# Fourier mixing and a gated convolution on one core: tables loaded in halves, part of the weight conversion on ScalarE

## The chip, the cores and the metric

The kernel runs on one core of a Trainium2 chip. The core has a tensor engine (PE, with weight loads shown as PEld), a vector engine (DVE), a scalar engine (ACT), GpSimd (POOL) and a sync engine (SP) that here only issues transfers. Each engine works through its own instructions in order; semaphores let one wait for another. The metric is the time of one execution on the device in microseconds (us).

## The reference, cut to what matters

```python
X = np.fft.fft(x, axis=1)             # x: 8 x 3136 x 256
X = np.fft.fft(X, axis=2)
x = X.real                            # goes into the second block
h = np.maximum(x @ w_in, 0.0)         # w_in: 256 x 1024
hp = pad(h, one zero row at either end of the sequence)
for k in range(3):
    conv_out += conv_w[k] * hp[:, k:k + S, :]
gate = 1.0 / (1.0 + np.exp(-conv_out))
out = (h * gate) @ w_out              # w_out: 1024 x 256
```

The weights come in as 64-bit floats and must be turned into 32-bit ones on the chip; x is 32-bit.

## The kernel before, in words

**The transform.** The Fourier transform along the sequence is done as matrix products with cosine and sine tables. Symmetry cuts the work: a sequence is first folded (`fold_ops`, on DVE, from tiles `xh`) into sums and differences over quarters of the sequence, in two halves h = 0 and 1 of four slots q, each from its own load of x (a plain transfer and four gathered ones that read mirrored rows). The folded values lie in two tiles `wt[b]`: one for even output frequencies, one for odd. The tables lie in `tabs[0]` (even) and `tabs[1]` (odd). ACT doubles the odd table by mirroring it (`mirror_tables(q)`, two slots at a time, L239) and halves one row (`mend_row`, L233). A `Unit` is a group of products into one PSUM tile, an ACT copy out of it and DVE additions (`fin`) that write the tiles `pt` (P) and `qt` (Q) in `PQ[b]`. The first batch has four odd units whose products are issued in four parts (parts 0 and 1 use slots 0 and 1, parts 2 and 3 slots 2 and 3), then four even units and one for a single feature column.

**The weights.** The transform along the features is merged into w_in: `blocks(i)` multiplies a quarter of w_in by the table `dm` into the matrix `G` (and one row into the tile `left`), `column(i)` makes the vector `ge`. The 64-bit weights are loaded as pairs of integers and converted by `narrow` with seven DVE instructions on 512 columns (L515 to L522): exponent cut out, rebased and clamped at zero, shifted into place, sign put in, mantissa's high word with its leading bit, low word added, product. w_in is narrowed in four quarters (`w_in[0]` to `w_in[3]`), w_out in four pieces of two blocks of rows (numbered 0, 2, 4, 6). Quarters 0 and 1 of w_in share one tile and their columns interleave; so do quarters 2 and 3.

**The steps.** Then come 256 steps (b, c, f): batch, one of four chunks of the sequence, one of eight blocks of 128 of the 1024 features. The loop is software pipelined and the order of all engines is written out by hand. In turn t it issues: sigmoid of step t-2 (ACT); the products of step t+1 (PE: `pb` = Q x G, `pa` = P x G, both 128 x 386) and their copies (ACT); the combination of step t (DVE, L686) into h, front and mirrored back of the chunk; side work; the seed of `pa` for step t+2 (ACT); the first tap of step t (ACT, L692), the other two taps of step t-1 (DVE, L698), the gate of step t-2 (half on POOL, L718, half on DVE, L719); and the output products of step t-3 (PE, `po`, `mm2`). Side work is hung into named places of a turn by `at(turn, place, function)`: "pe", "act", "dve", "load".

For the first 20 steps (`triple`), the front of h is not combined on DVE: PE adds a third product, Q x G again, into `pa` after `pb` has been read as the negative part, and ACT takes the front straight from PSUM by a Relu (L672). For the first four steps (`first`), the seed is a one-row product with `left` instead of an ACT activation.

**What sets the order at the start.** x goes out first on SP's queue, half 0 and then half 1 (the second behind a small POOL memset), then the odd tables (behind another memset, L575), quarter 0 of w_in, the even tables, `dm`, the other quarters. `keep_on(n)` is n idle products on PE (L748), which fill the time before the odd units. PE's wait for DVE or ACT is a count on that engine's semaphore.

Of the kernel before, what the change touches and what calls it, by code (L numbers as in the profile page):

```python
# [26 lines left out]

TRIPLE = 20  # L30
FIRST = 4
RC = 56
NQ = 8
# [5 lines left out]
def kernel(  # L39
# [22 lines left out]
    QO = HO // 2  # L62
    NF = F // P
# [6 lines left out]
    const = ctx.enter_context(tc.tile_pool(name="const", bufs=1))  # L70
# [19 lines left out]
    stt = nc.vector.scalar_tensor_tensor  # L90
    act = nc.scalar.activation

    def mm(o, l, r, start, stop):
        nc.tensor.matmul(o, l, r, start=start, stop=stop, skip_group_check=True)  # L94
# [12 lines left out]
    sg = const.tile([P, 2, 2], F32, name="sg")  # L107
# [96 lines left out]
    tabs = [const.tile([P, n, HQ, HE], F32, name="tab%d" % n) for n in (2, 4)]  # L204
    PQ, eb, er = {}, {}, {}
    ed = edp.tile([B, (RC // 2 + 1) * RC], F32, name="ed")

    def table(k, st, q, cols):
        return tabs[st // 2][0:k, st, q, cols] if st < 2 else tabs[1][0:k, st - 2, q, cols]

    def load_tables(par):


        st = slice(2 * par, 2 * par + 2)
        to = tabs[par][:, 0:2].rearrange("p s q i -> p s (q i)")
        n = HQ * HE
        m = NP // 2 // 16 * 16
        for i in range(2):
            nc.sync.dma_start(out=to[i:2 * m:2], in_=dft_seq[0:m, st, HQ * i:HQ * (i + 1)]
                              .rearrange("p s q i -> p s (q i)"))  # L220
        assert NP == 2 * m + 2
        nc.sync.dma_start(out=to[2 * m:NP], in_=bass.AP(
            tensor=dft_seq.tensor, offset=dft_seq.offset + (m * 4 + 2 * par) * NQ * HE,
            ap=[[n, 2], [NQ * HE, 2], [1, n]]))
        nc.sync.dma_start(out=to[NP:KR], in_=bass.AP(
            tensor=dft_seq.tensor, offset=dft_seq.offset + ((NP * 4 + 2 * par) * NQ - HQ + 2) * HE,
            ap=[[n, 1], [NQ * HE, 2], [1, n]]))

    def mend_row(par, half):
# [273 lines left out]
    left = const.tile([P, NF, P], F32, name="left")  # L503
# [1 line left out]

    def narrow(dst, raw):

        ts = nc.vector.tensor_scalar  # L510
        lsl, lsr = ALU.logical_shift_left, ALU.logical_shift_right
        lo, hi = raw[:, :, :, 0], raw[:, :, :, 1]
        lof, d = lo.bitcast(F32), dst.bitcast(I32)

        ts(out=d, in0=hi, scalar1=20, scalar2=0x7FF, op0=lsr, op1=ALU.bitwise_and)  # L515
        ts(out=d, in0=d, scalar1=-896, scalar2=0, op0=ALU.add, op1=ALU.max)
        ts(out=d, in0=d, scalar1=23, scalar2=None, op0=lsl)
        stt(out=d, in0=hi, scalar=-0x80000000, in1=d, op0=ALU.bitwise_and, op1=ALU.bitwise_or)

        ts(out=hi, in0=hi, scalar1=0xFFFFF, scalar2=0x100000, op0=ALU.bitwise_and, op1=ALU.bitwise_or)  # L520
        stt(out=lof, in0=lo.bitcast(U32), scalar=2.0 ** -32, in1=hi, op0=ALU.mult, op1=ALU.add)
        stt(out=dst, in0=lof, scalar=2.0 ** -20, in1=dst, op0=ALU.mult, op1=ALU.mult)  # L522

    class Weight:

# [7 lines left out]
        def load(self, eng):  # L533
            if self.raw is None:
                eng.dma_start(out=self.dst, in_=self.src)
            else:
                eng.dma_start(out=self.raw.rearrange("p c n e -> p c (n e)"), in_=self.src)

        def narrow(self, c0, c1):
            if self.raw is not None:  # L540
                narrow(self.dst[:, c0:c1], self.raw[:, c0:c1])

    ident = gp.tile([3 * NF, 3 * NF], F32, name="ident", tag="g")
    make_identity(nc, ident)
# [73 lines left out]
    hs, gs, pa, pb, po, nb = {}, {}, {}, {}, {}, {}  # L618
# [34 lines left out]
    def products(s):  # L653
        b, c, f = s
        ch, n, fs = cut(s)
        pb[s] = psb.tile([P, 512], F32, name="pb", tag="pb")
        mm(pb[s][:, 0:n], G[0:P - 1, 1, fs], PQ[b][1][0:P - 1, ch.k0:ch.k1], True, True)
        mm(pa[s][:, 0:n], G[:, 0, fs], PQ[b][0][:, ch.k0:ch.k1], first(s), not triple(s))
        if first(s):
            mm(pa[s][:, 0:n], left[0:1, f, :], er[b][:, ch.k0:ch.k1], False, False)  # L660
        if triple(s):
            mm(pa[s][:, 0:n], G[0:P - 1, 1, fs], PQ[b][1][0:P - 1, ch.k0:ch.k1], False, True)

# [36 lines left out]
    def shares(s):  # L700

        ch = chunks[s[1]]
        w = ch.w - 2
        n = ch.rest[0] if ch.last else w
        return slice(0, n // 2), slice(n // 2, n), slice(n, w)

    def sigmoid(s):

        v, p, r = shares(s)
        for c in (slice(p.start, r.stop), v):  # L710
            act(gs[s][:, c], gs[s][:, c], AF.Sigmoid)  # L711
# [36 lines left out]
    def keep_on(n):  # L748

        for _ in range(n):  # L750
            mm(idle[:, 0:2 * P], wt[0][1][0:NP, 1, 0], wt[0][1][0:NP, 0, 0:2], True, True)
# [54 lines left out]

# [40 lines left out]
    for b in range(1, B):  # L847
        ops = fold_ops(b)
        c0, n = ends[b - 1], ends[b] - ends[b - 1]
# [12 lines left out]
    n = len(steps)  # L862
# [4 lines left out]
    for t in range(n + LAG):  # L867
        def run(where):
            for fn in side.get((t, where), []):
                fn()  # L870
        if 0 <= t - 2 < n:
            sigmoid(steps[t - 2])
        if t + 1 < n:
            products(steps[t + 1])
            copies(steps[t + 1])
        run("act")
        if t < n:
            combine(steps[t])
# [12 lines left out]
        run("pe")  # L891
# [66 lines left out]
```

## Time and profile before

| what | before |
| --- | --- |
| time, median of 3 | 1218.17 us (1217.98 to 1218.82) |
| span of the profiled run | 1216.7 us |
| PE busy | 1185.4 us, 97% |
| DVE busy | 1125.0 us, 92% |
| ACT busy | 877.6 us, 72% |
| POOL busy | 373.2 us, 31% |
| chain that ended last | PE 70%, DVE 21%, issue 4%, ACT 2% |
| output products `po` on PE | 3072 passes, 380 ns mean |
| other taps (L698) on DVE | 512 instructions, 1073 ns mean |

A 32-bit matmul is run in two passes, each of which is one record; records overlap, since matmuls are pipelined, so a busy PE isn't PE at its peak. The chain that ended last is followed back from the last instruction, at each step to what released it. In the time lines a row has the start, the time it spans, engine, line, operation, output <- inputs, shape, count, and in brackets the idle time ahead of it and what ended that. Several like instructions are merged in one row. In the groups of waits, the time is that in which the waiting engine stood idle.

### The profile page before, as it was taken

Reading aid. Unit: us, or ns where it says so; the run is one execution under the profiler, and the core shown is the slowest. Engines: PE = TensorE matmul, PEld = TensorE weight load, DVE = VectorE, ACT = ScalarE, POOL = GpSimd, SP = SyncE. Lnnn points to the kernel's source line nnn. Section 1 sums busy time; section 2 is a strip of 40 time slices with the busy share of each in tenths; the row PEclk is TensorE's granted clock in tenths of the full one; section 3 lists DMA queues with packets and bytes.
Section 4 is the critical chain, followed back from the end, with each engine's and each line's share of the span. In section 5 each row is a group of like instructions: output and inputs, shape, how many; then the busy total and the mean of one; then the engine's idle time right before and its main releaser. Section 6 shows DMA issues by size and latency. Waiting matters only on the chain.

```text
span 1216.7 us, 15448 instructions
## 1 busy us (share of the span) xinstructions
PE 1185.4 (97%) x4876; PEld 906.4 (74%) x4876; DVE 1125.0 (92%) x1696; ACT 877.6 (72%) x1832; POOL 373.2 (31%) x474
## 2 busy tenths in 40 slices
PE   5999999999999999999999999999999999999998
PEld 4676777677777777777777777777777777777776
DVE  7799999999999999998999999999998988899996
ACT  2467656676777777777776777777777777788884
POOL 5224524343233232424224242332222222222222
PEclk9999999999999999999999999999999999999999
DMA  9622243211131110302121020310001000110000
GB/s 223 193 8 80 80 49 100 68 53 41 40 87 51 60 46 1 106 26 73 34 73 61 5 80 27 89 45 26 27 1 53 31 26 27 46 33 27 26 27 31
DMA packets 70213, 66.30 MB, mean 54 GB/s; under 512 B 28123, under 2 KB 57827, under 8 KB 70131
## 3 DMA queue, kind: packets, MB, share of 16 engines
q1 hardware_dynamic: 64493, 52.18, 15.3%
q0 software_dynamic: 5120, 12.85, 3.6%
q8 instruction: 39, 0.64, 0.2%
q14 instruction: 43, 0.35, 0.1%
q10 hardware_dynamic: 518, 0.28, 0.1%
HBM read 39.53 MB, written 25.74 MB: 54 GB/s over the span
## 4 chain that ended last, share of the span: by engine, by line
PE 70%; DVE 21%; issue 4%; ACT 2%; DMA 0%; DVEq 0%; SPq 0%; ACTq 0%
PE po L94 43%; PE pb L94 10%; PE pa L94 10%; DVE g L698 7%; PE pd L94 6%; DVE h L686 3%; DVE g L719 3%; DVE xh L158 2%; ACT nb L675 1%; DVE xh L169 1%; DVE w L186 1%; DVE w L187 1%; DVE xh L173 0%; DVE pt L291 0%; ACT g L711 0%
## 5 line engine op out<-in xcount | busy, mean ns | idle before, releaser
L94 PE MATMUL po<-wout,g 128*128 128x256 f32 x3072 | 709.0, 380 | 11.0 <-DVE g L719 10.3
L94 PEld LDWEIGHTS po<-wout,g 128*128 128x128 f32 x3072 | 578.6, 190 | 164.2 <-DVE g L719 43.6
L698 DVE SCALAR_TENSOR_TENSOR g<-h,cw,g 128x770 f32<-128x770 f32 (+1 forms) x512 | 549.4, 1073 | 9.3 <-ACT g L692 0.2
L718 POOL TENSOR_TENSOR g<-g,h 128x385 f32<-128x385 f32 (+1 forms) x256 | 233.9, 914 | 767.2 <-ACT g L711 485.6
L711 ACT ACTIVATE g<-g 128x385 f32<-128x385 f32 (+2 forms) x512 | 244.1, 526 | 191.8 <-DVE g L698 191.3
L675 ACT ACTIVATE nb<-pb 128x386 f32<-128x386 f32 (+2 forms) x472 | 207.9, 493 | 85.1 <-PE pb L94 84.1
L686 DVE CUSTOM_DVE_ANT_0 h<-pa,nb 128x386 f32<-128x386 f32 (+2 forms) x492 | 255.9, 560 | 3.7 <-ACT h L672 3.7
L692 ACT ACTIVATE g<-h,cw 128x770 f32<-128x770 f32 (+1 forms) x256 | 243.2, 950 | 0.2 <-DVE h L686 0.2
L94 PE MATMUL pb<-qt,G 127*128 127x387 f32 (+2 forms) x512 | 212.6, 496 | 0.0
L94 PE MATMUL pa<-pt,G 128*128 128x387 f32 (+2 forms) x512 | 211.8, 494 | 0.0
L641 ACT ACTIVATE pa<-eb,ge 128x387 f32<-128x387 f32 (+2 forms) x252 | 151.4, 601 | 1.3 <-PE pa L94 0.7
L94 PEld LDWEIGHTS pa<-pt,G 128*128 128x128 f32 x512 | 96.8, 189 | 73.6 <-issue 18.1
L719 DVE TENSOR_TENSOR g<-g,h 128x385 f32<-128x385 f32 (+1 forms) x256 | 146.3, 571 | 0.9 <-ACT g L711 0.9
L94 PE MATMUL pd<-tab,w 98*128 98x196 f32 (+3 forms) x448 | 126.7, 374 | 0.0
L133 POOL DMA_INDIRECT xh<-in_x_dram,idx x64 | 105.7, 1651 | 13.3 <-issue 9.2
L94 PEld LDWEIGHTS pb<-qt,G 127*128 127x128 f32 x512 | 94.0, 190 | 17.9 <-issue 1.4
L94 PEld LDWEIGHTS pd<-tab,w 98*128 98x128 f32 (+1 forms) x448 | 84.7, 191 | 12.3
L738 ACT COPY os<-po 128x256 f32<-128x256 f32 x196 | 57.5, 393 | 8.5 <-PE po L94 4.6
L158 DVE TENSOR_TENSOR xh<-xh 98x1020 f32<-98x1020 f32 (+1 forms) x32 | 40.7, 1279 | 2.3 <-DMA xh<-in_x_dram,idx 2.3
L169 DVE TENSOR_TENSOR xh<-xh 98x1024 f32<-98x1024 f32 (+1 forms) x32 | 41.3, 1292 | 0.1
L188 POOL COPY w<-xh 98x4 f32<-98x4 f32 (+1 forms) x32 | 19.6, 612 | 26.8 <-DVE xh L169 14.8
L291 DVE TENSOR_TENSOR qt<-as,pd 128x197 f32<-128x197 f32 (+1 forms) x14 | 7.2, 514 | 20.3 <-ACT as L287 20.3
(114 smaller groups left out, 394.0 us busy)
## 6 DMA issues: line engine op xcount, KB each, us to landing
out_dram<-os SPq DMA_DIRECT2D x192, 128.0 KB
xh<-in_x_dram SPq DMA_DIRECT2D x16, 784.0 KB
eb<-ed SPq DMA_DIRECT2D x16, 193.5 KB
tab<-dft_seq_dram SPq DMA_DIRECT2D x4, 589.5 KB
raw<-in_moe_w_in_dram SPq DMA_DIRECT2D x4, 512.0 KB
raw<-in_moe_w_out_dram SPq DMA_DIRECT2D x1, 2048.0 KB
eb<-ed SPq DMA_DIRECT2D x8, 209.0 KB
eb<-ed SPq DMA_DIRECT2D x8, 193.0 KB
```

The lines of the kernel that those rows point to most:

```text
L94: nc.tensor.matmul(o, l, r, start=start, stop=stop, skip_group_check=True)
L133: nc.gpsimd.indirect_dma_start(out=xh[b, h][0:NP, 7 - m].rearrange("p q d -> p (q d)"), out_offset=None, in_=bass.AP(tensor=x.tensor, offs ...
L158: vt(a[:, :, :, 1:D], a[:, :, :, 1:D], r[:, :, :, D - 1:0:-1], op=ALU.add)
L641: act(pa[s][:, 0:n], eb[b, c], AF.Copy, scale=ge[:, f:f + 1])
L675: act(nb[s][:, i, cols], p[:, cols], AF.Copy, scale=-1.0 if i else 1.0)
L686: nc.vector._custom_dve(TENSOR_ADD_SAT, out=to, in0=a[:, cols], in1=c[:, i, cols], s0=BIG, s1=0.0)
L692: act(gs[s], hs[s][:, 0:n], AF.Copy, scale=cw[:, 0, s[2]:s[2] + 1])
L698: stt(out=g, in0=h[:, k:k + n], scalar=cw[:, k, f:f + 1], in1=g, op0=ALU.mult, op1=ALU.add)
L711: act(gs[s][:, c], gs[s][:, c], AF.Sigmoid)
L718: gt(g[:, p], g[:, p], h[:, p], op=ALU.mult)
L719: vt(g[:, v], g[:, v], h[:, v], op=ALU.mult)
L738: nc.scalar.copy(out=osb[:, j % 2], in_=pt[:, j % 2])
```

## The change

It has three parts, all before or at the beginning of the steps.

1. The odd tables are loaded in two halves (slots 0 and 1, then 2 and 3), each queued directly behind its half of x, so that the first parts of the odd units can go ahead with the first half. The idle products on PE are split: eight before part 0 and six between parts 1 and 2, in place of sixteen ahead of all. Quarter 0 of w_in is narrowed after the odd units instead of before them, quarter 1 after the even ones.
2. For six narrowings (quarters 2 and 3 of w_in, all four of w_out) the rebasing, clamping and shifting of the exponent is one ACT activation, Relu(2^23 x exponent - 896 x 2^23), in place of two DVE instructions. Such a narrowing falls into `power` (one DVE instruction and the activation), hung into a new place "first" between sigmoid and products of a turn, and `product` (four DVE instructions), which stays in the place "dve". The mantissa's high word goes to a spare part of the tile `left`, since the sign is still to be read. Quarters 2 and 3 move to turns 0 and 1.
3. `triple` no longer holds for steps 0, 1 and 2: they go without the third product on PE, and DVE combines their fronts.

```diff
-TRIPLE = 20
+TRIPLE = 3, 20
...
-    def load_tables(par):
+    def load_tables(par, q0, q1):
...
-        to = tabs[par][:, 0:2].rearrange("p s q i -> p s (q i)")
-        n = HQ * HE
+        to = tabs[par][:, 0:2, q0:q1].rearrange("p s q i -> p s (q i)")
+        n = (q1 - q0) * HE
...
+    low = const.tile([P, 1], F32, name="low")
+    nc.gpsimd.memset(low, -896.0 * 2 ** 23)
...
-    def narrow(dst, raw):
+    def narrow(dst, raw, room=None):
...
+        def power():
+
+            ts(out=d, in0=hi, scalar1=20, scalar2=0x7FF, op0=lsr, op1=ALU.bitwise_and)
+            if room is not None:
+                act(d, d, AF.Relu, scale=2.0 ** 23, bias=low[0:d.shape[0]])
+            else:
+                ts(out=d, in0=d, scalar1=-896, scalar2=0, op0=ALU.add, op1=ALU.max)
+                ts(out=d, in0=d, scalar1=23, scalar2=None, op0=lsl)
...
+        def product():
+
+            if room is None:
+                sign()
+            ts(out=sg, in0=hi, scalar1=0xFFFFF, scalar2=0x100000, op0=ALU.bitwise_and, op1=ALU.bitwise_or)
+            stt(out=lof, in0=lo.bitcast(U32), scalar=2.0 ** -32, in1=sg, op0=ALU.mult, op1=ALU.add)
+            if room is not None:
+                sign()
+            stt(out=dst, in0=lof, scalar=2.0 ** -20, in1=dst, op0=ALU.mult, op1=ALU.mult)
+        return power, product
...
     for h in range(2):
         for f in load_ops(0, h, nc.sync, nc.scalar, h == 1):
             f()
-
-    nc.gpsimd.memset(tabs[1][0:1, 0, 0, 0:1], 0.0)
-    load_tables(1)
+        nc.gpsimd.memset(tabs[1][0:1, 0, 2 * h, 0:1], 0.0)
+        load_tables(1, 2 * h, 2 * h + 2)
     w_in[0].load(nc.sync)
-    load_tables(0)
+    load_tables(0, 0, HQ)
...
-        return s[0] == 0 and s[1] * NF + s[2] < TRIPLE
+        return s[0] == 0 and TRIPLE[0] <= s[1] * NF + s[2] < TRIPLE[1]
...
     odds = [us[j] for j in (0, 1, 5, 6)]
-    w_in[0].narrow(0, 2)
-    keep_on(16)
+    keep_on(8)
     mirror_tables(0)
     mend_row(1, half)
     mirror_tables(2)
     for i in range(4):
+        if i == 2:
+            keep_on(6)
         for j, u in enumerate(odds):
...
     mend_row(0, half)
-    w_in[1].narrow(0, 2)
+    w_in[0].narrow(0, 2)
     for i, u in enumerate(us[j] for j in (2, 4, 3, 7, 8)):
         u.matmuls(0, 1)
         u.copy()
         u.fin()
+    w_in[1].narrow(0, 2)
...
     blocks(0)
-    w_in[2].narrow(0, 2)
...
-    at(0, "dve", lambda: w_in[3].narrow(0, 2))
+
+    room = left[:, NF // 2:].rearrange("p f i -> p (f i)").bitcast(I32)
+
+    def shared(cycle, w, c):
+        for where, fn in zip(("first", "dve"), w.parts(c, c + 2, room)):
+            at(cycle, where, fn)
+
+    for i in (2, 3):
+        shared(i - 2, w_in[i], 0)
...
     for cycle, c in ((2, 0), (3, 2), (5, 4), (7, 6)):
-        at(cycle, "dve", lambda c=c: w_out.narrow(c, c + 2))
+        shared(cycle, w_out, c)
...
             sigmoid(steps[t - 2])
+        run("first")
         if t + 1 < n:
             products(steps[t + 1])
             copies(steps[t + 1])
```

More of the change, by code (lines that the diff above doesn't have):

```diff
@@ L209, in table @@
         return tabs[st // 2][0:k, st, q, cols] if st < 2 else tabs[1][0:k, st - 2, q, cols]
-    def load_tables(par):
+    def load_tables(par, q0, q1):
         st = slice(2 * par, 2 * par + 2)
-        to = tabs[par][:, 0:2].rearrange("p s q i -> p s (q i)")
-        n = HQ * HE
+        to = tabs[par][:, 0:2, q0:q1].rearrange("p s q i -> p s (q i)")
+        n = (q1 - q0) * HE
         m = NP // 2 // 16 * 16
         for i in range(2):
-            nc.sync.dma_start(out=to[i:2 * m:2], in_=dft_seq[0:m, st, HQ * i:HQ * (i + 1)]
+            nc.sync.dma_start(out=to[i:2 * m:2], in_=dft_seq[0:m, st, HQ * i + q0:HQ * i + q1]
                               .rearrange("p s q i -> p s (q i)"))
@@ L222, in load_tables @@
         nc.sync.dma_start(out=to[2 * m:NP], in_=bass.AP(
-            tensor=dft_seq.tensor, offset=dft_seq.offset + (m * 4 + 2 * par) * NQ * HE,
-            ap=[[n, 2], [NQ * HE, 2], [1, n]]))
+            tensor=dft_seq.tensor, offset=dft_seq.offset + ((m * 4 + 2 * par) * NQ + q0) * HE,
+            ap=[[HQ * HE, 2], [NQ * HE, 2], [1, n]]))
         nc.sync.dma_start(out=to[NP:KR], in_=bass.AP(
-            tensor=dft_seq.tensor, offset=dft_seq.offset + ((NP * 4 + 2 * par) * NQ - HQ + 2) * HE,
+            tensor=dft_seq.tensor, offset=dft_seq.offset + ((NP * 4 + 2 * par) * NQ - HQ + 2 + q0) * HE,
             ap=[[n, 1], [NQ * HE, 2], [1, n]]))
@@ L513, in narrow, with sign @@
         lof, d = lo.bitcast(F32), dst.bitcast(I32)
[L515 to L522, printed above, removed]
+        sg = hi
+        if room is not None:
+            c, n = hi.shape[1:]
+            sg = room[:, 0:c * n].rearrange("p (c n) -> p c n", c=c)
+        def power():
[5 more added lines that the diff above has]
+                ts(out=d, in0=d, scalar1=23, scalar2=None, op0=lsl)
+        def sign():
+            stt(out=d, in0=hi, scalar=-0x80000000, in1=d, op0=ALU.bitwise_and, op1=ALU.bitwise_or)
+        def product():
[3 more added lines that the diff above has]
+            stt(out=lof, in0=lo.bitcast(U32), scalar=2.0 ** -32, in1=sg, op0=ALU.mult, op1=ALU.add)
+            if room is not None:
+                sign()
+            stt(out=dst, in0=lof, scalar=2.0 ** -20, in1=dst, op0=ALU.mult, op1=ALU.mult)
+        return power, product
     class Weight:
@@ L537, in load, with parts @@
                 eng.dma_start(out=self.raw.rearrange("p c n e -> p c (n e)"), in_=self.src)
+        def parts(self, c0, c1, room=None):
+            if self.raw is None:
+                return []
+            return narrow(self.dst[:, c0:c1], self.raw[:, c0:c1], room)
         def narrow(self, c0, c1):
-            if self.raw is not None:
-                narrow(self.dst[:, c0:c1], self.raw[:, c0:c1])
+            for f in self.parts(c0, c1):
+                f()
     ident = gp.tile([3 * NF, 3 * NF], F32, name="ident", tag="g")
@@ L657, in products @@
         mm(pb[s][:, 0:n], G[0:P - 1, 1, fs], PQ[b][1][0:P - 1, ch.k0:ch.k1], True, True)
-        mm(pa[s][:, 0:n], G[:, 0, fs], PQ[b][0][:, ch.k0:ch.k1], first(s), not triple(s))
+        mm(pa[s][:, 0:n], G[:, 0, fs], PQ[b][0][:, ch.k0:ch.k1], first(s), not first(s) and not triple(s))
         if first(s):
-            mm(pa[s][:, 0:n], left[0:1, f, :], er[b][:, ch.k0:ch.k1], False, False)
+            mm(pa[s][:, 0:n], left[0:1, f, :], er[b][:, ch.k0:ch.k1], False, not triple(s))
         if triple(s):
```

## The prediction

> **What bounds the kernel now.** I read four views in this order: busy time by stretches, the waits of the tensor engine, the chain that ended last in order of time, and the time lines of the first 65 us. Everything the change touches runs before 95 us, so the busy time there comes first (columns: stretch, length, busy PE, PEld, DVE, ACT, POOL, granted clock, DMA share, GB/s).
>
> ```profile
> 20.00:30.00 10.00, 10.00 (x42) 7.92 (x42) 9.40 (x15) 5.06 (x10) 2.95 (x4) 1.00 1.05 219
> 40.00:50.00 10.00, 10.00 (x37) 5.54 (x36) 8.86 (x20) 3.98 (x9) 5.39 (x10) 1.00 0.73 229
> 60.00:70.00 10.00, 10.00 (x40) 6.33 (x40) 9.66 (x16) 7.50 (x16) 2.36 (x3) 1.00 0.49 5
> 90.00:100.00 10.00, 8.55 (x34) 6.03 (x33) 9.87 (x12) 5.48 (x12) 3.18 (x3) 1.00 0.30 84
> 110.00:120.00 10.00, 8.43 (x32) 5.62 (x31) 9.90 (x12) 6.92 (x18) 4.90 (x8) 1.00 0.20 60
> ```
>
> PE looks full early, but from 60 us DVE has no gaps and from 90 us PE does. What PE waits for over the whole span (us, times, longest):
>
> ```profile
> PE po L94 <- DVE g L719: 10.3, 20, 1.9
> PE pb L94 <- POOL w L188: 8.6, 1, 8.6
> ```
>
> The chain says where the hand-over from PE to DVE is (start, us, what):
>
> ```profile
> 54.51 2.35 PE pa L94 x6
> 56.90 0.04 issue
> 56.94 0.50 ACT h L672
> 57.44 0.02 issue
> 57.47 0.56 DVE h L686
> 58.03 0.34 DVE wout L515
> ```
>
> Until step 2 is combined at 57.47 us the end is set by PE, and from there to 148 us by an unbroken run of DVE instructions. So a microsecond more or less before 57.47 on PE, and after it on DVE, moves the end; later everything shifts as a block. The rows of the start:
>
> ```profile
> 15.27 10.24 PE L94 MATMUL pb<-w 98*128 98x256 f32 x32 [8.56 <-POOL w L188]
> 25.35 8.10 PE L94 MATMUL po<-tab,w 98*128 98x196 f32 x32
> ...
> 41.07 2.85 PE L94 MATMUL po<-win,dm 128*128 128x256 f32 x12
> 43.85 0.92 PE L94 MATMUL pb<-qt,G 127*128 127x386 f32 x2
> ```
>
> ```profile
> 35.58 0.42 DVE L515 TENSOR_SCALAR win<-raw 128x512 int32<-128x512 int32 x1
> ...
> 42.75 0.41 DVE L515 TENSOR_SCALAR win<-raw 128x512 int32<-128x512 int32 x1
> ...
> 47.72 0.56 DVE L686 CUSTOM_DVE_ANT_0 h<-pa,nb 128x385 f32<-128x385 f32 x1 [0.83 <-ACT h L672]
> ...
> 48.65 0.43 DVE L516 TENSOR_SCALAR win<-win 128x512 int32<-128x512 int32 x1
> 49.11 0.43 DVE L517 TENSOR_SCALAR win<-win 128x512 int32<-128x512 int32 x1
> 49.57 0.69 DVE L518 SCALAR_TENSOR_TENSOR win<-raw,win 128x512 int32<-128x512 int32 x1
> ```
>
> ```profile
> 23.18 1.96 ACT L239 ACTIVATE tab<-tab 99x392 f32<-99x392 f32 x4 [16.26 <-DMA tab<-dft_seq_dram]
> ...
> 60.47 1.28 ACT L711 ACT_TABLE_LOAD   x1
> ```
>
> **What the Trainium skill says.** (1) "TensorE: Matmul & The Clock Gate", Part 1: the array runs at half clock until it has been busy for a window of about 3.4 us, and falls back after an idle one; windows run freely. The trace agrees with the first half: the keep-on matmuls last 634 ns each at 17 to 20 us and 379 ns at 22 to 24 us. At 2.59 us for the twelve 256-column passes of a step, a warm pass takes 0.216 us, a half-clock one 0.43; 32 passes in 10.08 us make 15 slow ones, so it stayed slow for 6.3 us after an idle 8.6. The granted clock shows 1.00 throughout and does not record this. No PE gap of 2 to 6 us exists in this trace, so it doesn't show what one does. (2) "ScalarE: Activation LUTs", What ACT_TABLE_LOAD costs: 1283 ns for a table load, 280 ns + 0.833 ns per element for an activation with a pointer bias. The trace has 1.28 us. (3) "SBUF — State Buffer", Who interferes with whom: a DVE instruction with two SBUF inputs contends with GpSimd reads. The pair of taps takes 2.07 us alone and 2.56 us at 61.85, when POOL gates at 62.44: 0.5 us per gate.
>
> **The change part by part.**
>
> *Tables in halves.* Before, ACT gets all odd tables at 23.18. In the built program ACT's first mirror instruction, for half 0, waits for half 0 and also for the first three transfers of half 1. So the order of arrival helps only if half 1 is early. It is issued at the same place (12.96 us) with half the bytes; I put its landing at 19 to 23.2 us (before, 1.2 MB took from 12.96 to 23.18). Mirroring takes 1.96, so part 1 of the odd products can start at 21 to 25.2. PE: the first 16 keep-on passes end where the 17th began, 15.27 + 15 x 0.43 + 0.2 = 21.9; part 0 (a quarter of 7.94) ends at 23.9. So PE waits 0 to 1.3 us; I take 0. Four passes fewer in all are 4 x 0.216 = 0.86 us, less 0.1 for two more POOL memsets: even products begin **0.75 us earlier** (33.6).
>
> *Narrowing of quarters 0 and 1 moved back.* Before, quarter 0 was narrowed at 25.72, while DVE had nothing else, quarter 1 at 35.58, and blocks(0) found both done. Now quarter 0 takes the slot at 35.58 and quarter 1 the one at 42.75 (where quarter 2 was), after the eight `fin` operations. In the built program the second matmul of blocks(0) waits for the DVE count that the last instruction of quarter 1 reaches: the two quarters interleave in one tile, and the wait covers both. That instruction ends at 46.89 - 0.75 = 46.1. PE finishes the even products at 41.07 - 0.75 = 40.3 and one block matmul at 40.75, then **stands idle 5.4 us**. Behind the waiting matmul are all of blocks(0) and steps 0 and 1; ACT waits for its G copies, DVE for step 0. From the second block matmul to the end of step 0's three remaining products the trace has 41.51 (two passes of 0.22 after 41.07) to 46.19 (43.85 and three pairs), 4.68 us: 50.8; with 0.3 to drain and signal, combine(0) starts at 51.1, against 47.72.
>
> *The clock.* An idle of 5.4 us is longer than the window, so I expect PE cold again. Then 3.4 to 6.8 us at half rate cost 1.7 to 3.4; I take **2.5**; lower end 0, if no whole window falls into the gap (5.4 - 3.4 of 3.4 gives at least 0.6 that one does; partly idle windows may do too: 0.67).
>
> *Steps 0 to 2, warm.* Third products: three pairs of 0.75 us leave PE, 2.25 in all; DVE gains three combines of 0.47 (start to start), ACT swaps a Relu of 0.49 for a copy of 0.49. A narrowing loses the two instructions between 48.65 and 49.57, 0.92 us, keeping 0.46 ahead of the combine and 2.53 after it. DVE from combine(0): 0.94 + 2.53 + 0.46 + 0.94 + 2.53 + 0.6 (quarter 3's exponents stand on ACT behind the copies of blocks(1) and column(0)) + taps 1.98 + 0.46 = 10.4, so combine(2) starts at 51.1 + 10.4 = 61.5: **+4.0**, against 57.47.
>
> *A new wait in step 2.* The sign of the first output narrowing waits for ACT's Relu of the exponents, which stands on ACT behind two `ge` copies, the table load and sigmoid(0). PE's blocks(2) need quarter 3 narrowed (59.2) and take with both columns 3.7 us: 62.9. Then copies 0.3, load 1.28, sigmoid 0.94, the Relu 0.65 (between 0.49 for 385 and 0.93 for 770 elements): 66.1. DVE is there at 61.5 + 0.94 + 0.46 + 0.73 = 63.7. **+2.4**, behind which taps and gates queue; one POOL gate now falls into this wait, -0.5. Bounds 0 and 2.4.
>
> *Output narrowings.* Four times 0.92, and 0.46 of the first already spent, minus the third combine 0.47: **-3.7** by combine(8). The other Relus cost nothing: DVE needs 1.7 us from the exponents to the sign, ACT is free by then.
>
> Sum: 4.0 + 2.4 - 0.5 - 3.7 = +2.2 warm, +4.7 cold. PE itself is late by only 4.8 - 2.25 (+2.5) and led DVE by 5.3 us at step 8 (its inputs stood ready at 88.5 us and were combined at 93.82), so DVE keeps setting the time.
>
> **Rivals.** (A) The clock survives the gap: 1218.2 + 2.2 = **1220.4**. For it: windows run freely; against: 5.4 us. (B) Clock warm and ACT ready in step 2: +2.2 - 1.9 = +0.3, **1218.5**. For it: ACT was only 75% busy; against: in-order copies. (C) The relief wins, faster: if the block wait is not felt, 0.75 earlier, and DVE saves 6 x 0.92 - 3 x 0.47 = 4.1: 1218.2 - 4.9 = **1213.3**. For it: DVE is at 99% from 60 to 148 us; against: the wait is in the program and DVE's order is fixed.
>
> **How the numbers follow.** Main case, cold: 1218.2 + 4.7 = **1222.9**, chance 0.5; A 0.25, B 0.15, C 0.1. The bound of 0.2% is 2.4 us (1215.8 and 1220.6). Slower: 0.95 of main, 0.45 of A: 0.59. Faster: C, 0.1. Same: 0.31. Range: from B less 1 us, 1217.5, to main with cold 0.9 longer and tables late by 1.3, about 1225.5; C and a tail are left out.
>
> **What would show it.** Right: PE idle for about 5 us before the blocks at 46 us, released by the last narrowing instruction; then block matmuls near 600 ns; combine(0) at 51 to 54; a DVE wait of some 2 us for ACT ahead of a sign in step 2; DVE narrowings of 3.0 us; combine(8) 2 to 5 us later than 93.82. Wrong: no gap at 41 us, or odd products held by tables beyond 25 us, or PE setting the chain after step 8.

## The result, and the profile after

The changed kernel takes 1223.35 us (median of 4, 1222.3 to 1225.2), beside 1218.08 us before (1217.69 to 1218.82): slower, ratio 1.0044 with a 95% interval of 1.0027 to 1.0062. The profiled run of the changed kernel took 1222.3 us, its span is 1220.5 us (before: 1216.7).

Four starts locate the difference. I name the first instruction that combines step n on DVE combine(n); before it is L686, after it L713.

| start, us | before | after | later by |
| --- | --- | --- | --- |
| even products (PE, first 197-column row) | 34.35 | 34.94 | 0.59 |
| combine(0) | 47.72 | 54.28 | 6.56 |
| combine(2) | 57.47 | 64.81 | 7.34 |
| combine(8) | 93.82 | 97.51 | 3.69 |
| from combine(8) to the end of the span | 1122.9 long | 1123.0 long | |

So 6 us are lost between the even products and combine(0), 0.8 more up to combine(2), and 3.65 come back up to combine(8). Nothing behind it changes: in the changed kernel and in all twelve kernels of the experiments, the span ends 1122.8 to 1123.1 us behind combine(8).

The busy time of the same stretches of the changed kernel (columns as before):

```profile
20.00:30.00 10.00, 8.28 (x35) 6.24 (x35) 8.66 (x11) 4.98 (x10) 2.63 (x4) 1.00 1.04 245
40.00:50.00 10.00, 4.80 (x19) 3.71 (x17) 7.54 (x17) 1.94 (x4) 6.00 (x11) 0.72 0.70 235
60.00:70.00 10.00, 10.00 (x44) 6.31 (x44) 6.52 (x12) 7.12 (x15) 0.87 (x1) 1.00 0.01 2
90.00:100.00 10.00, 10.00 (x42) 7.62 (x41) 9.86 (x14) 7.89 (x16) 2.21 (x3) 1.00 0.29 82
```

PE, full before, has holes in the first two stretches, and in the second the granted clock is 0.72. DVE, full before from 60 us, has 3.5 us of holes in the third. From 90 us it is full again. The waits of PE and then of DVE, from 20 to 100 us (us, times, longest):

```profile
PE po L94 <- DVE win L543: 5.2, 1, 5.2
PE po L94 <- ACT tab L239: 1.7, 1, 1.7
PE po L94 <- ACT tab L233: 0.9, 1, 0.9
```

```profile
DVE h L713 <- ACT win L527: 6.5, 1, 6.5
...
DVE wout L533 <- ACT wout L527: 2.4, 1, 2.4
DVE win L533 <- ACT win L527: 1.0, 1, 1.0
```

Of these, only the 0.9 us wait was there before. The 6.5 us of DVE is the far side of PE's 5.2: DVE has done the narrowing and waits for step 0. (The releaser printed, the Relu on ACT, ended just ahead of it and is not what held it: combine(0) reads the products of step 0, and in a_dve_narrow below, which has no Relu, the same wait is 7.48 us and put down to PE.) Where these waits lie, in the time lines of PE, ACT and DVE (start, us, engine, line, what, idle time ahead and its end):

```profile
21.37 2.14 PE L94 MATMUL po<-tab,w 98*128 98x196 f32 x8
25.23 2.25 PE L94 MATMUL po<-tab,w 98*128 98x196 f32 x8 [1.72 <-ACT tab L239]
27.31 2.75 PE L94 MATMUL pb<-w 98*128 98x256 f32 x12
29.90 4.14 PE L94 MATMUL po<-tab,w 99*128 99x196 f32 x16
34.94 1.67 PE L94 MATMUL po<-tab,w 99*128 99x197 f32 x8 [0.90 <-ACT tab L233]
...
41.67 0.59 PE L94 MATMUL po<-win,dm 128*128 128x256 f32 x2
47.47 4.30 PE L94 MATMUL po<-win,dm 128*128 128x256 f32 x10 [5.20 <-DVE win L543]
```

```profile
23.27 1.90 ACT L239 ACTIVATE tab<-tab 99x392 f32<-99x392 f32 x4 [16.32 <-DMA tab<-dft_seq_dram]
```

```profile
65.74 0.42 DVE L539 TENSOR_SCALAR left<-raw 128x512 int32<-128x512 int32 x1
66.19 0.69 DVE L540 SCALAR_TENSOR_TENSOR raw<-raw,left 128x512 f32<-128x512 uint32 x1
69.24 0.69 DVE L533 SCALAR_TENSOR_TENSOR wout<-raw,wout 128x512 int32<-128x512 int32 x1 [2.35 <-ACT wout L527]
```

The first mirroring on ACT begins at 23.27 us, no earlier than with whole tables (23.18). The second block matmul waits 5.20 us for L543, the last instruction of quarter 1's narrowing; the blocks' ten passes behind it take 4.30 us, 0.43 each, where all twelve took 2.85 before. The clock around it (two-microsecond stretches; the first figure after POOL's count is the granted clock):

```profile
44.00:46.00 2.00, 0.00 (x0) 0.00 (x0) 1.86 (x5) 0.00 (x0) 1.39 (x3) 0.59 0.48 157
46.00:48.00 2.00, 0.53 (x1) 0.50 (x2) 1.72 (x3) 0.00 (x0) 1.10 (x5) 0.50 0.59 141
48.00:50.00 2.00, 2.00 (x6) 1.35 (x4) 0.00 (x0) 0.37 (x1) 0.00 (x0) 0.50 0.63 216
50.00:52.00 2.00, 2.00 (x6) 0.63 (x6) 0.00 (x0) 0.57 (x2) 0.00 (x0) 0.70 0.94 308
```

A mean of 0.59 from 44 to 46 us makes 0.36 us at 1.00 and the rest at 0.50: the clock falls at about 44.4 us, 2.1 us after PE went idle at 42.27. By the same sum it comes back at about 51.2. The chain that ended last then runs over ACT in step 2 (start, us, what):

```profile
46.72 0.70 DVE win L543
47.42 0.04 issue
47.47 4.30 PE po L94 x10
...
66.19 0.16 ACT ge L636
66.35 0.02 issue
66.37 1.28 ACT L738
67.65 0.01 issue
67.66 0.94 ACT g L738 x2
68.60 0.62 ACT wout L527
69.24 0.70 DVE wout L533
```

After the narrowing and the blocks, PE carries the chain to 66.2 us; then `ge` copy, table load, sigmoid and Relu on ACT; only from 69.24 is it DVE.

### The profile page after: what moved, and what is told of

Read it like the earlier page. It is cut to its first block, busy times and chain, and to the rows that moved or that the text cites. A ratio compares the mean times of both kernels' runs of the same rounds, so it can differ in the third digit from the quotient of the medians.

```text
span 1220.5 us, 15438 instructions
## 1 busy us (share of the span) xinstructions
PE 1183.7 (97%) x4866; PEld 905.1 (74%) x4866; DVE 1118.9 (92%) x1687; ACT 881.9 (72%) x1838; POOL 372.6 (31%) x476
## 4 chain that ended last, share of the span: by engine, by line
PE 70%; DVE 21%; issue 4%; ACT 2%; DMA 1%; POOL 1%; SPq 0%; DVEq 0%; POOLq 0%; ACTq 0%
PE po L94 43%; PE pb L94 11%; PE pa L94 10%; DVE g L725 7%; PE pd L94 6%; DVE h L713 3%; DVE g L746 3%; DVE xh L158 2%; ACT nb L702 1%; DVE xh L169 1%; DVE w L186 1%; DMA tab<-dft_seq_dram 1%; DVE w L187 1%; POOL xh L133 1%; DMA xh<-in_x_dram 0%
## 5 line engine op out<-in xcount | busy, mean ns | idle before, releaser
L702 ACT ACTIVATE nb<-pb 128x386 f32<-128x386 f32 (+2 forms) x478 | 210.8, 493 | 86.3 <-PE pb L94 85.3
L713 DVE CUSTOM_DVE_ANT_0 h<-pa,nb 128x386 f32<-128x386 f32 (+2 forms) x495 | 257.0, 559 | 6.5 <-ACT win L527 6.5
```

The source lines that it names most:

```text
L702: act(nb[s][:, i, cols], p[:, cols], AF.Copy, scale=-1.0 if i else 1.0)
L713: nc.vector._custom_dve(TENSOR_ADD_SAT, out=to, in0=a[:, cols], in1=c[:, i, cols], s0=BIG, s1=0.0)
```

## The experiments

My theory was the prediction's: the wait of the blocks for quarter 1 costs most, the half clock behind it adds some 2 us, the Relus and the missing third products give about 4 us back. The first rival was that DVE, busy either way, sets the time whatever PE waits for; the second, which came from the trace of the changed kernel, that the tables in halves themselves cost time. Twelve kernels were run in three groups (a, b, c), each beside the kernel before, which took 1218.68, 1218.42 and 1218.45 us in them. Group a ran on another chip than b and c, so kernels of different groups are compared by their distance from their own before.

| kernel | time, us (runs) | ratio to before, 95% interval | even products at | from there to combine(0) | combine(0) to (8) |
| --- | --- | --- | --- | --- | --- |
| before | 1218.08 to 1218.68 | 1 | 34.35 | 13.37 | 46.10 |
| changed | 1223.35 (4) | 1.0044 [1.0027, 1.0062] | 34.94 | 19.34 | 43.23 |
| a_layout | 1217.05 (13) | 0.9986 [0.9978, 0.9995] | 35.33 | 12.79 | 42.56 |
| a_warm | 1222.87 (7) | 1.0032 [1.0021, 1.0044] | 37.21 | 17.63 | 43.24 |
| a_dve_narrow | 1232.54 (4) | 1.0117 [1.0101, 1.0132] | 39.15 | 20.02 | 48.48 |
| a_triple | 1226.44 (5) | 1.0065 [1.0051, 1.0079] | 37.28 | 21.10 | 43.91 |
| b_tabs | 1224.06 (5) | 1.0045 [1.0032, 1.0059] | 37.32 | 19.38 | 43.24 |
| b_both | 1215.26 (20) | 0.9981 [0.9975, 0.9988] | 34.99 | 12.79 | 42.54 |
| b_lay_whole | 1213.96 (6) | 0.9967 [0.9955, 0.9979] | 33.91 | 12.72 | 42.64 |
| b_only23 | 1214.20 (6) | 0.9966 [0.9954, 0.9978] | 33.35 | 12.92 | 43.36 |
| c_sep | 1222.16 (5) | 1.0035 [1.0021, 1.0048] | 34.05 | 19.01 | 43.23 |
| c_whole | 1222.26 (8) | 1.0032 [1.0021, 1.0043] | 34.82 | 20.12 | 43.28 |
| c_whole_warm | 1219.93 (21) | 1.0013 [1.0006, 1.0020] | 35.10 | 17.63 | 43.28 |
| c_only23_early | 1213.62 (5) | 0.9961 [0.9948, 0.9975] | 34.50 | 12.84 | 42.18 |

The last three columns are of the profiled run, the time is a median over all. When the even products begin varies between runs of one kernel too, so the columns behind it say more of an edit than the time does.

**a_layout: take away what makes the blocks wait for quarter 1.**

```diff
-    win = [pqp.tile([P, NK], F32, name="win", tag=tag)[:, 0:F].rearrange("p (t n) -> p t n", t=2)
+    win = [pqp.tile([P, NK], F32, name="win", tag=tag)[:, 0:F].rearrange("p (i t n) -> p i t n", i=2, t=2)
...
-    w4 = [win[i // 2][:, :, i % 2 * N4:(i % 2 + 1) * N4] for i in range(4)]
+    w4 = [win[i // 2][:, i % 2] for i in range(4)]
```

> The changed kernel with the quarters of w_in stored one after the other in their tile, so that the wait of blocks(0) covers quarter 0 alone; order and instructions are the same. Theory (the block wait and the cold array behind it are the loss): no PE gap before the blocks, no half-rate passes, step 0 combined at 47.7 us instead of 54.28, step 8 near 90.5 instead of 97.5, and 1214.8 us, faster than before by some 3.3. Rival 1 (the loss is the hand-over of exponents to ScalarE): the blocks start early, but DVE waits longer for ACT, 1221 or more. Rival 2 (late tables and the late second fold): at most 1.3 us come back, 1222.

1217.05 us. In its time line of PE, the blocks run in one go, and no clock is lost:

```profile
42.06 2.84 PE L94 MATMUL po<-win,dm 128*128 128x256 f32 x12
```

From the even products to combine(0) it takes 12.79 us instead of 19.34, so 6.55 us of the loss are this wait and what it does to the clock. The wait was only a matter of layout: the same instructions in the same order, with the two quarters no longer interleaved. DVE had no less to do, so the first rival falls. In the profiled run combine(0) and combine(8) came at 48.12 and 90.68 us, near the 47.7 and 90.5 expected. The median stayed 2.2 us above the expectation, and the mean granted clock of each run gives a hint why: the seven runs with 0.999 or 1.000 have a median of 1215.5 us, the six with 0.998 one of 1217.8. That mean doesn't say where in a run PE was at half rate, and by itself it isn't proof (the kernel before has runs with 0.996 at 1217.99 to 1219.74 us, beside a median of 1218.45). But it fits a loss of clock ahead of the even products in some runs, as the next experiment's trace shows one.

**a_warm and c_whole_warm: the same wait, with a busy array.** In the time in which PE waits it does 11 idle products. a_warm is the changed kernel with this edit, c_whole_warm is c_whole (below) with it.

```diff
+    keep_on(11)
     blocks(0)
```

> The changed kernel with eleven idle products ahead of blocks(0), which end before its second matmul is released, so that the array has work in the gap; the wait itself stays. Theory (the array turns cold in the gap and pays about 1.9 us for it): blocks at the full rate, step 0 combined near 52.4 us, 1221.4 us, and runs closer together than 2.9 us, since the phase of the clock's window no longer counts. Rival (the half rate is hidden behind DVE's work): 1223.3.

> c_whole with 11 keep-on products before the blocks, in the time in which PE waits for the last narrowing instruction: the wait is as long, the array is busy in it. a_warm was the same on the changed kernel, but fell to half rate before the odd products in its profiled run, which hid the effect. Theory (the half rate behind the block wait costs 1.9 us): blocks to the end of step 0's products 4.7 us instead of 6.6, 1218.6 us. Rival (DVE has slack there, the clock is hidden): as c_whole, 1220.5 us.

Of a_warm, the time would say that the clock is worth nothing (1222.87 against 1223.35 us). Its trace says why not. Combine(0) comes 17.63 us behind the even products instead of 19.34: 1.71 us won, about the 1.9 expected. But the even products begin 2.27 us later, since in this run the array fell to half rate once before, behind a longer wait for the mirrored tables. PE's line of part 1, and the clock of two stretches:

```profile
25.80 3.36 PE L94 MATMUL po<-tab,w 98*128 98x196 f32 x8 [2.28 <-ACT tab L239]
```

```profile
26.00:28.00 2.00, 2.00 (x7) 1.61 (x7) 1.97 (x4) 1.97 (x5) 0.14 (x1) 0.70 1.02 220
28.00:30.00 2.00, 2.00 (x5) 1.20 (x4) 1.84 (x3) 0.85 (x2) 1.31 (x2) 0.50 0.99 217
```

By the sum used above the clock fell at 26.8 us, when PE was at work again for 1 us. So the comparison was repeated without that wait. c_whole_warm beside c_whole: 1219.93 against 1222.26 us, 2.3 us, with intervals that do not meet (1219.93 is 1.3 above its expectation, as c_whole is 1.8 above its own). Blocks and step 0 run at full rate in it:

```profile
46.57 0.60 PE L94 MATMUL po<-win,dm 128*128 128x256 f32 x2
47.70 2.52 PE L94 MATMUL po<-win,dm 128*128 128x256 f32 x10 [0.53 <-DVE win L543]
```

The half clock behind the block wait is worth about 2 us, and DVE does not hide it. Both rivals of these two runs fall.

**a_dve_narrow: all six narrowings wholly on DVE.**

```diff
-        for where, fn in zip(("first", "dve"), w.parts(c, c + 2, room)):
-            at(cycle, where, fn)
+        at(cycle, "dve", lambda: w.narrow(c, c + 2))
```

> The changed kernel with all six exponents back on DVE: seven DVE instructions for each narrowing, in the place where four stood. Theory (the share on ScalarE is a gain that is partly given back in two waits): DVE has 6 x 0.92 us more and loses the waits of 0.99 and 2.35; step 2 combined 1.2 us later, step 8 about 3, 1226.3 us. Rival (the hand-over is the loss): 1220.5 or less.

1232.54 us, 6 us above the expectation. Combine(0) to combine(8) takes 48.48 us instead of 43.23: 5.25 us more, where about 3 were expected. The two waits for ScalarE are gone, as expected: behind combine(0) DVE doesn't wait any more. So without the 3.3 us of waits DVE has 8.6 us more to do, 1.4 for each narrowing, where the prediction had 0.92. ScalarE's share is worth more than was said. A narrowing takes 3.90 us from its first instruction to the next tap (these two lines), where in the changed kernel it takes 2.74 without the combine inside it and the gates:

```profile
64.97 0.42 DVE L525 TENSOR_SCALAR win<-raw 128x512 int32<-128x512 int32 x1
...
68.87 2.07 DVE L725 SCALAR_TENSOR_TENSOR g<-h,cw,g 128x770 f32<-128x770 f32 x2
```

What the prediction had left out, the order of the instructions and where the gates fall, stands below, under combine(2) to combine(8). The rest of the time is the start again: PE's wait for the tables was 3.16 us and the even products began at 39.15, 4.2 later than in the changed kernel.

**a_triple: the third products back in steps 0 to 2.**

```diff
-TRIPLE = 3, 20
+TRIPLE = 0, 20
```

> The changed kernel with the third product in steps 0 to 2 again. Theory (PE is on the path until step 2's first narrowing): PE has 3 x 0.75 us more, DVE three combines of 0.47 less; the sign of the first output narrowing comes 2.2 us later, 1225.3 us. Rival (the three added combines cost DVE): 1222.

1226.44 us. From the even products to combine(0) it takes 1.76 us longer: one third product of 0.75 us and the Relu behind it, and some 0.4 us because the half clock lasted longer in this run (until 54.4 us, 4.5 us into the blocks, instead of 3.7). From there to combine(8) it takes 0.68 longer. So to leave them out helps, by some 2 us in the profiled runs; the rest of the difference in time is the later start (37.28).

**b_tabs and c_sep: does the first mirroring wait for the wrong half?** In the built program ACT's first mirror instruction waits for half 0 and also for three transfers of half 1. Two ways to end that: b_tabs splits the odd tile by halves, c_sep makes it two tiles.

```diff
-    tabs = [const.tile([P, n, HQ, HE], F32, name="tab%d" % n) for n in (2, 4)]
+    tabs = [const.tile([P, 2, HQ, HE], F32, name="tab2")]
+    halves = [const.tile([P, 4, 2, HE], F32, name="tabh%d" % h) for h in range(2)]
```

(c_sep, with every use of the odd tables changed to match; b_tabs has one tile, viewed as two halves.)

> The changed kernel with one edit: the odd table tile is laid out half by half, so that the first mirroring no longer waits for transfers of half 1. Theory (the halves of the tables gain nothing because the first mirroring waits for half 1, and in some runs the array then falls to half rate): the wait of PE ahead of part 1 is gone, parts 0 and 1 run on end to end, even products begin near 33.2 us instead of 34.9, everything later follows: 1221.0 us (1219.5 to 1221.7). Rival (half 1's arrival sets part 2 in any case, so the wait only moves behind part 1): even products still at 34.5 or later, 1223 us.

> The changed kernel with one edit: the odd tables lie in two tiles, one for each half, so that the first mirroring can wait for half 0 alone (b_tabs dropped only one of the three transfers of half 1 from that wait). Theory (the wait of PE ahead of part 1, and the half-rate spell that follows it in some runs, come from that covering wait): the first mirroring runs before 19 us, parts 0 and 1 run end to end at about 21.5 to 25.7, part 2 starts between 28.3 and 29.0 (second half of x folded) and even products at 33.3 to 34.0 instead of 34.9: 1221.3 us, with less spread between runs. Rival (half 0 itself lands as late as 23 us): no change, 1223.5.

b_tabs changed nothing: 1224.06 us, the mirroring still at 23.95. Its built program shows that the edit missed its aim: of the three waits for half 1, two were left. Those transfers write every other partition, and stay tied to the other half as long as both lie in one tile. So b_tabs says nothing on the theory. In c_sep the waits are gone, and the lines of ACT and PE are the ones that the change was after (the second line of ACT is the first that waits for half 1):

```profile
14.78 1.91 ACT L241 ACTIVATE tabh<-tabh 99x392 f32<-99x392 f32 x4 [8.11 <-DMA tabh<-dft_seq_dram]
23.89 1.13 ACT L234 ACTIVATE tabh<-tabh,half 2x393 f32<-2x393 f32 x2 [7.20 <-DMA tabh<-dft_seq_dram]
```

```profile
22.45 4.13 PE L94 MATMUL po<-tabh,w 98*128 98x196 f32 x16
26.41 2.75 PE L94 MATMUL pb<-w 98*128 98x256 f32 x12
29.00 4.14 PE L94 MATMUL po<-tabh,w 99*128 99x196 f32 x16
34.05 1.67 PE L94 MATMUL po<-tab,w 99*128 99x197 f32 x8 [0.91 <-ACT tab L234]
```

The mirroring runs 8.5 us earlier, parts 0 and 1 are one piece. From the start of part 0 to the even products it takes 11.60 us instead of 13.57, 2.0 us less. But PE's idle products ahead of part 0 began 0.3 us later and ran at half rate for longer in this run, so that part 0 starts 1.1 us later. The runs lie no closer together than before (1221.1 to 1224.6), and the time, 1222.16 us, can't be told from the changed kernel's: the ratios are 1.0035 [1.0021, 1.0048] and 1.0044 [1.0027, 1.0062].

**b_both: both layouts** (a_layout with b_tabs).

> The changed kernel with both layouts: quarters of w_in contiguous, odd tables half by half, so that neither covering wait is left. Theory: the two add; a_layout's 1217.05 us less 1.7 (the wait) and less another 1 on average for the runs in which the array fell to half rate: 1214.5 us, combine(0) near 46.4, combine(8) near 89. Rival (DVE's in-order work after 46 us takes the gain back): 1216.5 to 1217.

1215.26 us with even products at 34.99: since b_tabs does nothing, this is a_layout measured once more, with a table wait of 0.74 us in the profiled run where a_layout had 1.22. It isn't the test that it was meant to be. Its 20 runs fall into the same two groups: 13 with a mean clock of 0.999 or 1.000 and a median of 1215.2 us, seven with 0.997 or 0.998 and 1217.3.

**b_lay_whole and c_whole: tables as before.** Whole odd tables behind both halves of x, 16 idle products ahead of part 0, none between; once on a_layout, once on the changed kernel.

```diff
-        load_tables(1, 2 * h, 2 * h + 2)
+    load_tables(1, 0, HQ)
...
-    keep_on(8)
+    keep_on(16)
...
-        if i == 2:
-            keep_on(6)
```

> a_layout with the transfers and the odd products as in the kernel before: both halves of x, then whole odd tables, 16 keep-on passes and no 6 between. Theory (part 1 of the change, the tables in halves, costs time by itself): even products at 34.3 instead of 35.3 us and no half-rate spell before them: 1215.5 us. Rival (the halves are neutral): 1217.0 us.

> The changed kernel with tables and odd products as in the kernel before (both halves of x, whole odd tables, 16 keep-on passes); quarters 0 and 1 still narrowed late, so that the block wait stays. Theory (part 1 of the change costs 3 us, as between a_layout and b_lay_whole): even products at 33.4 to 34.3 us, no half-rate spell before them, the block wait of about 5.2 us at 41 us with the half rate behind it: 1220.5 us. Rival (without the block layout the loss of the halves is hidden by DVE's narrowing of quarter 1): 1223 us.

b_lay_whole: 1213.96 us, 1.5 less than expected and 4.5 below its before, where a_layout is 1.6 and b_both 3.2 below theirs. No run of it has a mean clock under 0.999. PE's odd products run in one piece and end earlier:

```profile
24.91 8.10 PE L94 MATMUL po<-tab,w 98*128 98x196 f32 x32
33.91 1.67 PE L94 MATMUL po<-tab,w 99*128 99x197 f32 x8 [0.90 <-ACT tab L233]
```

So the second rival holds in part: the first part of the change costs time by itself where nothing else hides it. On the changed kernel (c_whole, 1222.26 us) it is 1.1 us in the medians, less than the 2.8 expected, and the intervals overlap; in its profiled run the block wait was as long as in the changed kernel (5.28 us), but the half clock lasted longer (combine(0) 20.12 us behind the even products instead of 19.34).

**b_only23: the second and third part alone, on the kernel before.** Quarters 0, 1 and 2 are narrowed where that kernel does. Written as an edit of c_whole:

```diff
+    w_in[0].narrow(0, 2)
     keep_on(16)
...
-    w_in[0].narrow(0, 2)
+    w_in[1].narrow(0, 2)
...
-    w_in[1].narrow(0, 2)
     flip()
...
     blocks(0)
+    w_in[2].narrow(0, 2)
...
-    for i in (2, 3):
-        shared(i - 2, w_in[i], 0)
+    shared(0, w_in[3], 0)
```

> The kernel before with the second and third part of the change alone: Relu of exponents on ScalarE for quarter 3 and the four output narrowings, no third product in steps 0 to 2; tables whole, quarters 0, 1 and 2 narrowed where the kernel before does. Theory: no block wait, combine(0) near 47.1 us, combine(2) near 54.7 (set by PE, 2.25 us of third products less), then the 32.7 us that the changed kernel takes to combine(8): 87.4 us, 6.4 earlier than before, 1212 us. Rival (the step 2 wait for ScalarE grows as DVE comes earlier, or PE takes over as the bound): 1215 to 1217 us.

1214.20 us: better than both kernels, but 2 us above the expectation and no better than b_lay_whole. Combine(2) did come early, at 53.87, but from there to combine(8) it took 35.76 us, 3.1 more than the 32.7 expected. Of these, 2.1 are the wait for ScalarE, which grew from 2.35 to 4.44 us, as the rival said; 0.9 is one pair of taps in step 6 that took 3.49 us instead of 2.55, for which the trace shows no cause.

```profile
53.87 1.02 DVE L714 CUSTOM_DVE_ANT_0 h<-pa,nb 128x385 f32<-128x385 f32 x2 [0.95 <-PE pa L94]
...
60.40 0.69 DVE L533 SCALAR_TENSOR_TENSOR wout<-raw,wout 128x512 int32<-128x512 int32 x1 [4.44 <-ACT wout L527]
```

**c_only23_early: the first output exponents one step earlier.**

```diff
     for cycle, c in ((2, 0), (3, 2), (5, 4), (7, 6)):
-        shared(cycle, w_out, c)
+        power, rest = w_out.parts(c, c + 2, room)
+        at(1 if cycle == 2 else cycle, "dve" if cycle == 2 else "first", power)
+        at(cycle, "dve", lambda f=rest: f())
```

> b_only23 with one edit: the exponents of the first output narrowing go to ScalarE one step earlier, ahead of the ge copies, the table load and the sigmoid of step 0. Theory (the wait of 4.44 us for ScalarE's Relu in step 2 moves the end): the wait is gone, combine(3) is then set by its products and the bias copy near 61.5 us instead of 64.5, 3 us saved: 1211.2 us. Rival (the gates on GpSimd that ran in the wait now contend with taps, and PE ends the next wait): 1213 us or more.

1213.62 us, 2.4 above the expectation, the lowest time of all, though not told apart from b_only23 and b_lay_whole. DVE's lines show where the 4.4 us went:

```profile
57.02 0.68 DVE L533 SCALAR_TENSOR_TENSOR wout<-raw,wout 128x512 int32<-128x512 int32 x1
...
60.94 0.99 DVE L747 TENSOR_TENSOR g<-g,h 128x385 f32<-128x385 f32 x1 [0.52 <-ACT g L739]
...
66.59 0.69 DVE L533 SCALAR_TENSOR_TENSOR wout<-raw,wout 128x512 int32<-128x512 int32 x1 [2.77 <-ACT wout L527]
```

The sign of the first output narrowing no longer waits. The gate then waits 0.5 us for the sigmoid, and the sign of the second narrowing, one step on, 2.8 us for its Relu. From combine(2) to combine(3) 3.5 us are won (7.16 instead of 10.66), up to combine(4) 2.7 of them are lost again, and up to combine(8) 1.2 are left. The rival holds. As I read it, the work that ends last in steps 2 and 3 runs through PE and ACT, and DVE meets it one way or another.

## Why the prediction was right, and where it was not

The forecast, 1222.9 us, slower, was right, and so was its main mechanism. Some of its terms were wrong, in directions that cancel, so that it came within 0.5 us of the measured 1223.35 is partly luck.

- **Tables in halves: wrong.** The step said PE would wait 0 to 1.3 us ahead of part 1, took 0, and had the even products 0.75 us earlier. The wait was 1.72 us, outside the bounds, and they came 0.59 later. What failed is that half 1, with half the bytes, was given a landing from 19 us on. In c_sep ACT waits for half 1 until 23.89 us, as late as for the whole tables (23.18 before, 24.21 in c_whole), while half 0 had landed by 14.78. The covering wait that the prediction had found in the program thus made half 0 as late as half 1. Why half 1 is so late is argued only: the transfers' share was at its full already (1.05 from 20 to 30 us in the view shown before), and by its end the same bytes have to be through as before, both halves of x and all odd tables. Besides, part 0 ended at 23.5 us, 0.4 earlier than reckoned, which made the wait longer.
- **The wait of the blocks: right.** Idle 5.4 us, released by the last narrowing instruction of quarter 1; measured 5.20. That instruction ended 1.3 us later than the 46.1 of the prediction, as the even products came 1.3 later than its 33.6. a_layout shows that the layout is the cause, which the prediction had read from the program alone.
- **The clock: right, a little smaller.** 2.5 us foreseen, with 0 to 3.4 as bounds. From 47.47 us to the end of step 0's products it took 6.56 us instead of 4.68: 1.9 us; 2.3 between c_whole_warm and c_whole. Rival A falls with that. No whole idle window was needed: of the 3.4 us ahead of the fall PE was idle for 2.1. The prediction had allowed for partly idle windows without being able to show them.
- **Combine(0) and (2): right in sum.** Cold, they were put at 53.6 and 64.0; 54.28 and 64.81 were measured, later by the tables' miss less the smaller loss of clock.
- **The wait for ScalarE in step 2: right.** 2.4 us foreseen, 2.35 measured, behind just the named queue: `ge` copies, table load, sigmoid. The wait for quarter 3's exponents was put at 0.6 and is 0.99. Rival B, in which ACT is ready, falls. But the prediction took the wait as a cost of its own. c_only23_early speaks against that, on b_only23: take it away there and 1.2 us are won of 4.4.
- **Combine(2) to combine(8): right sign, too small.** Predicted +2.4 - 0.5 - 3.7 = -1.8, measured -3.65. Two terms are missing. The gates on GpSimd cost DVE some 1.0 us less than I let them: before, six fell onto taps and onto narrowing instructions at about 0.5 us each (L517 took 0.98 us once instead of 0.43, L521 1.24 instead of 0.69); after, one falls into the wait, two onto taps, and three onto L539, which goes up by just 0.2 (0.65 us between starts instead of 0.45). And the new order saves some 0.8 us that I did not count. In these lines an instruction whose successor needs its result takes 0.1 us longer from start to start: L540, now ahead of an instruction that doesn't need it, takes 0.61 us instead of L521's 0.72, and L525 0.34 instead of L515's 0.45.
- **The sum.** At combine(8) I had +4.7 and the trace has +3.69. The median of the runs is 5.3 us above before, 1.1 us more than the profiled run. A half-rate spell ahead of the even products, as a_warm, a_dve_narrow, a_triple and b_tabs have it, would do that in some runs; the profiled run of the changed kernel itself doesn't show one, so this stays an inference. It fits that the longest of its four runs, 1225.2 us, has the lowest mean clock, 0.995.
- **Rival C**, 1213.3 us if the block wait is not felt, counted on tables 0.75 us earlier. With the wait gone and the tables still in halves it is 1217.05 us (a_layout). Only with whole tables as well is it 1213.96 (b_lay_whole), so the near hit is not that of rival C's sum.

By the medians, the loss of 5.3 us is made up of: relief on DVE and PE by the second and third part, -4.5 (b_lay_whole); the block wait with a warm array, +5.9 (c_whole_warm less b_lay_whole, each from its own before; in the profiled runs 5.6 of it lie behind the start of the even products); the clock behind it, +2.3 (c_whole less c_whole_warm); the tables in halves, +1.5 (changed less c_whole, which the intervals don't secure). Two of three parts of the change were good; the first, and the places that it gave to the narrowings of quarters 0 and 1, undid them. Of the 2.8 us by which a_layout stays behind b_lay_whole, each from its own before, 1.3 are left when only its runs with a mean clock of 0.999 or more are taken, about the longer way to the even products (1.4 us in the profiled runs). The rest goes with the runs of a lower clock. That those lost it ahead of the even products stays open, since none of them has a trace.

## What to carry to other kernels

When two pieces of work are to be told apart by time, lay them out apart: quarters or halves that interleave in one tile were waited for together here, and the built program shows it before any run. For the quarters of w_in it was enough to store one after the other (a_layout); for the halves of the tables it took two tiles (c_sep), since one tile with the halves one after the other kept two of three waits (b_tabs). A transfer of half the size, at the same place in the order behind full DMA engines, landed no earlier than the whole (23.89 in c_sep, 23.18 before). After taking a wait away, look for the next one on the same chain, and compare single stages rather than whole times where a wait ahead of them varies.

## What the runs showed of the hardware

- The array lost its full rate in shorter gaps than the prediction had reckoned with. It took the idle window from the Trainium skill, "TensorE: Matmul & The Clock Gate", Part 1, some 3.4 us; the runs differ, and the measurement decides: gaps that are too short to hold a whole window of that length did it. Every stretch at half rate that the granted clock shows in the first 60 us of a profiled run lasted 3.4 us or twice that (44.4 to 51.2 us in the changed kernel, 26.8 to 30.2 in a_warm), and in the 3.4 us ahead of each fall PE was idle for 2.1 to 3.4. So the fall can come after the gap. Ahead of part 1 the same work waited for different times in seven profiled runs:

| kernel | PE idle, us | part 1, eight passes, us |
| --- | --- | --- |
| b_both | 0.74 | 2.25 |
| a_layout | 1.22 | 2.25 |
| changed | 1.72 | 2.25 |
| a_warm | 2.28 | 3.36 |
| a_triple | 2.44 | 3.12 |
| b_tabs | 2.99 | 3.94 |
| a_dve_narrow | 3.16 | 4.29 |

  Up to 1.72 us it stayed warm, from 2.28 us on it went to half rate. That makes the first part of the change worse than its wait: in the last four of these runs the even products begin 2.3 to 4.2 us later than in the changed kernel's.
- The granted clock does record the fall after such a gap (0.50), but shows 1.00 from 16 to 20 us in the changed kernel, while idle products start 0.427 us apart there, 0.216 later. The first stretch at half rate of a run isn't in it.
- The Relu of 128 x 512 on ScalarE took 0.70 to 0.72 us; the prediction had taken 0.65.
